# Linformer attention and a hard-swish feed-forward layer: key and value projections in two column tiles of the array

**Chip, cores, metric.** One Trainium2 chip (trn2), one core. The metric is the device time of one execution in microseconds, as the median of the executions of a kernel.

## The reference, cut to what matters

```python
# q, k, v: (8 batches, 8 heads, 1024 positions, 64); E, F: (64, 1024); fp32 in and out
k_proj = np.einsum('ks,bhsd->bhkd', E, k)          # 1024 positions -> 64
v_proj = np.einsum('ks,bhsd->bhkd', F, v)
attn = softmax(q @ k_proj.transpose(0, 1, 3, 2) / 8)
x = (attn @ v_proj)                                # -> (8192, 512)
h = x @ w_in                                       # 512 -> 2048
out = (h * np.clip(h + 3, 0, 6) / 6) @ w_out       # 2048 -> 512
```

## The kernel before

It computes in bf16. The attention of batch b+1 is a generator. The feed-forward layer of batch b calls it for one step after every group of four first-layer matmuls (called F below; not the matrix F) and after every group of sixteen second-layer matmuls (called S). The order of the steps is thereby the order of TensorE's instructions.

```python
ef_t = consts.tile([P, 2, SO, 2, KP], bf16, name="ef_t")   # E^T, F^T, each twice: 128 columns
...
def attention(b, xT):
    ...
    def project(e, src):
        ps = pat()                                   # one PSUM bank, from a ring of 4
        for so in range(SO):                         # SO = 8, KP = 64
            nc.tensor.matmul(ps, ef_t[:, e, so].rearrange("p a m -> p (a m)"), src[:, :, so, :],
                             start=(so == 0), stop=(so == SO - 1))
            if so == SO // 2 - 1:
                yield
        res[e] = ps
    res = {}
    yield from project(0, kt)
    kp = att.tile([KP, H, 2, D], bf16, tag="kp", name="kp")
    k_ps = res[0].rearrange("p (h d) -> p h d", h=H)
    for a in range(2):
        nc.vector.tensor_copy(kp[:, :, a, :], k_ps[:KP])
    yield
    yield from project(1, vt)
    vp = att.tile([P, H, D], bf16, tag="vp", name="vp")
    nc.vector.tensor_copy(vp.rearrange("p h d -> p (h d)"), res[1])
    yield
    kt_ps = pat().bitcast(bf16)[:, :H * KP]
    ...                                              # 8 transposes of kp, 2 copies into kbd
    yield
    ...                                              # q_transpose(0), scores(0), ..., values, normalise
...
for t in range(NB):                                  # NB = 2, in each batch
    ...
    for fo in range(FO):                             # FO = 16
        first_group(xT, t, g, fo)                    # F: 4 matmuls, a Relu, a VectorE product
        next(steps, None)
        if prev is not None and fo % SB == SB - 1:   # SB = 4
            second_group(*prev, fo // SB)            # S: 16 matmuls, a copy, a store
            next(steps, None)
```

The softmax here doesn't subtract the row's maximum and nothing guards it: scores larger than these inputs give would overflow.

## Time and profile before

| | before |
|---|---|
| median time | 575.63 us (574.79 to 576.09, 3 runs) |
| TensorE busy | 532.7 us of a span of 573.1 us |
| 16 projection matmuls of a steady batch | 3.45 us |
| period of a steady batch | 66.26 us |

The *period* is the time from the first projection matmul of one batch to that of the next. It is 66.26 us five times in a row (from 103.05 to 434.35 us). The profile has no records for some 50 of the feed-forward matmuls, which shows as a count of 3 where the program has 4 and costs no time. The profile's lines are shown in the prediction. Their numbers (in brackets those of the changed kernel, where they differ): L126 the projections, L145 (L142) the transposes of kp, L159 (L156) those of q, L163 (L160) the copy into qT, L169 (L166) the scores, L177 (L174) the denominators and values, L214 (L211) F, L217 and L218 (L214 and L215) its Relu and product, L223 (L220) S. A row of the timeline has start and length in us, engine, line, operation, and the idle time ahead of it with what ended it. PE is TensorE, PEld its weight loads, DVE VectorE, ACT ScalarE and POOL GpSimd; 128*64 are the rows and columns of the array that a matmul uses. A mean duration of a matmul in the groups (381 ns) is not its cost: matmuls overlap, and what counts is the step from one start to the next, 0.216 us at full clock.

### The profile page before, as it was taken

To read this page: it belongs to the slowest core of one execution; us is meant where nothing else is said; L and a number is where in the kernel's file an instruction comes from. 1 tells how busy PE (TensorE), PEld (TensorE's weight loads), DVE (VectorE), ACT (ScalarE), POOL (GpSimd) and SP (SyncE) were. 2 spreads that over 40 slices of the span, in tenths; PEclk is the share of its full clock that TensorE was granted. 3 is DMA by queue.
4 is the path that set the end of the run, shared out by engine and by line. 5 is a ranking of instruction groups with operands and counts; after the bars stand their busy time and mean duration, and the time that the engine had idled before them with its cause. 6 is when DMAs were issued, how large, how long until landed. Compare 5 with 4: busy or idle time off the path is not lost.

```text
span 573.1 us, 7173 instructions
## 1 busy us (share of the span) xinstructions
PE 532.7 (93%) x2770; PEld 240.3 (42%) x2824; DVE 254.4 (44%) x400; ACT 302.9 (53%) x513; POOL 28.9 (5%) x40
## 2 busy tenths in 40 slices
PE   2656999999999999999999999999999999999997
PEld 1212444444444444444444444444444444444443
DVE  1342764354535454535544454345444544444420
ACT  0261876366644665356743576437653666544431
POOL 6221000100001000100001000000000000000000
PEclk9887999999999999999999999999999999999999
DMA  9999992552419150380507333000110000011011
GB/s 137 207 206 207 209 214 70 96 106 51 97 38 157 46 102 28 68 153 19 111 37 119 84 74 75 37 20 37 38 37 19 38 37 20 38 51 40 38 38 74
DMA packets 38595, 46.87 MB, mean 82 GB/s; under 512 B 1568, under 2 KB 30240, under 8 KB 38560
## 3 DMA queue, kind: packets, MB, share of 16 engines
q0 software_dynamic: 29344, 29.62, 32.8%
q1 hardware_dynamic: 9216, 16.78, 7.6%
q8 instruction: 22, 0.36, 0.3%
q14 instruction: 13, 0.11, 0.1%
HBM read 59.24 MB, written 16.78 MB: 133 GB/s over the span
## 4 chain that ended last, share of the span: by engine, by line
PE 86%; DMA 8%; DVE 2%; ACT 1%; issue 1%; POOL 1%; ACTq 0%; POOLq 0%
PE mm L223 38%; PE mm L214 37%; DMA v<-in_v_dram 4%; PE at L126 4%; DMA w_in_sb<-in_moe_w_in_dram 4%; PE at L177 3%; PE at L169 2%; PE at L159 2%; DVE g L218 1%; ACT r L217 1%; DVE qT L163 1%; PE at L145 0%; POOL v L78 0%; POOL q L78 0%; POOL k L78 0%
## 5 line engine op out<-in xcount | busy, mean ns | idle before, releaser
L218 DVE SCALAR_TENSOR_TENSOR g<-r,mm 128x512 bf16<-128x512 f32 x256 | 175.5, 686 | 227.4 <-ACT r L217 226.8
L214 PE MATMUL mm<-xT,w_in_sb 128*128 128x512 bf16 x982 | 241.2, 381 | 3.0 <-DVE xT L193 1.0
L223 PE MATMUL mm<-w_out_sb,g 128*128 128x512 bf16 x1012 | 230.0, 379 | 0.6
L217 ACT ACTIVATE r<-mm,half 128x512 f32<-128x512 f32 x256 | 176.8, 691 | 73.6 <-PE mm L214 72.0
L223 PEld LDWEIGHTS <-g 128*128 128x128 bf16 x1024 | 99.8, 98 | 119.3
L214 PEld LDWEIGHTS <-w_in_sb 128*128 128x128 bf16 x1024 | 96.6, 98 | 120.3 <-issue 13.1
L226 ACT COPY o_sb<-mm 128x512 f32<-128x512 f32 x64 | 37.5, 587 | 164.7 <-PE mm L223 161.9
L193 DVE TENSOR_TENSOR xT<-at,rec 128x512 bf16<-128x512 f32 x64 | 43.5, 685 | 22.1 <-ACT rec L192 22.1
L170 ACT ACTIVATE aT<-at 128x512 bf16<-128x512 f32 x64 | 35.0, 609 | 25.6 <-PE at L169 25.6
L192 ACT ACTIVATE rec<-ln 128x512 f32<-128x512 f32 x64 | 40.6, 641 | 0.0
L187 ACT ACTIVATE ln<-at 128x512 f32<-128x512 f32 x64 | 34.6, 596 | 2.2 <-PE at L177 2.2
L126 PE MATMUL at<-k,ef_t 128*128 128x512 bf16 x64 | 18.8, 426 | 14.4 <-DMA k<-in_k_dram 14.4
L163 DVE COPY qT<-at 128x1024 bf16<-128x1024 bf16 x32 | 22.0, 686 | 16.4 <-PE at L159 16.2
L126 PEld LDWEIGHTS <-ef_t 128*128 128x128 bf16 x128 | 13.2, 104 | 36.1 <-issue 11.5
L169 PE MATMUL at<-qT,kbd 128*128 128x512 bf16 x64 | 19.9, 387 | 6.8 <-DVE qT L163 6.2
L159 PE MATMUL at<-ident,q 128*128 128x128 bf16 x256 | 20.0, 222 | 3.2 <-DVE xT L193 1.7
L159 PEld LDWEIGHTS <-q 128*128 128x128 bf16 x256 | 17.2, 99 | 12.0 <-issue 3.5
L126 PE MATMUL at<-v,ef_t 128*128 128x512 bf16 x64 | 17.7, 407 | 1.7 <-DMA v<-in_v_dram 1.5
L177 PE MATMUL at<-aT,ones 64*64 64x512 bf16 x128 | 14.2, 406 | 1.3 <-ACT aT L170 1.1
L177 PE MATMUL at<-aT,vp 64*64 64x512 bf16 x128 | 14.8, 385 | 0.2
L78 POOL DMA_DIRECT2D k<-in_k_dram x8 | 7.0, 881 | 140.6 <-PE at L126 137.0
L78 POOL DMA_DIRECT2D q<-in_q_dram x8 | 7.0, 880 | 140.1 <-PE at L159 136.0
(27 smaller groups left out, 63.3 us busy)
## 6 DMA issues: line engine op xcount, KB each, us to landing
out_dram<-o_sb SPq DMA_DIRECT2D x64, 256.0 KB, 2.0
k<-in_k_dram POOLq DMA_DIRECT2D x8, 1024.0 KB, 9.7
v<-in_v_dram POOLq DMA_DIRECT2D x8, 1024.0 KB, 12.9
q<-in_q_dram POOLq DMA_DIRECT2D x8, 1024.0 KB, 11.1
w_in_sb<-in_moe_w_in_dram POOLq DMA_DIRECT2D x4, 512.0 KB, 21.9
w_out_sb<-in_moe_w_out_dram POOLq DMA_DIRECT2D x4, 512.0 KB, 24.4
ef_raw<-in_E_dram POOLq DMA_DIRECT2D x1, 128.0 KB, 3.0
ef_raw<-in_F_dram POOLq DMA_DIRECT2D x1, 128.0 KB, 3.0
```

Source lines behind the costliest of these rows:

```text
L126: nc.tensor.matmul(ps, ef_t[:, e, so].rearrange("p a m -> p (a m)"), src[:, :, so, :], start=(so == 0), stop=(so == SO - 1))
L159: nc.tensor.transpose(ps[:, o:o + P], qt[:, 2 * j + a, 2 * m:2 * m + 2, :].rearrange("p s d -> p (s d)"), ident)
L170: nc.scalar.activation(aT[j][:, a, :], ps, AF.Exp, scale=scale)
L177: nc.tensor.matmul(tiles[t][c:c + D], stationary(r, 2 * j + a), aT[j][r:r + KP, a, :], start=True, stop=True)
L187: nc.scalar.activation(lns[t], den[t], AF.Ln)
L192: nc.scalar.activation(rec, ln, AF.Exp, scale=-1.0)
L193: nc.vector.tensor_mul(xT[:, j, t, :], av, rec)
L214: nc.tensor.matmul(h_ps, w_in_sb[:, ko, fo * P:(fo + 1) * P], xT[:, ko, t, :], start=(ko == 0), stop=(ko == KO - 1))
L217: nc.scalar.activation(r, h_ps, AF.Relu, bias=half[:], scale=1.0 / 6.0)
L218: nc.vector.scalar_tensor_tensor(g[:, fo, :], r, 1.0, h_ps, op0=ALU.min, op1=ALU.mult)
L223: nc.tensor.matmul(o_ps, g[:, fo, c * P:(c + 1) * P], w_out_sb[:, fo, :], start=(fo == 0), stop=(fo == FO - 1))
L226: nc.scalar.copy(o_sb, o_ps)
```

## The change

The stationary operand of a projection was E or F twice, 128 columns wide, so that the result lay in both halves of the partitions. Now it is 64 columns wide. k's result goes to partitions 0 to 63 and v's to 64 to 127 of one bank, by two column tiles (columns 0 to 63 and 64 to 127 of the array) that are meant to run at the same time. vp, which must be in both halves, is copied twice. One step falls away.

```diff
-    ef_t = consts.tile([P, 2, SO, 2, KP], bf16, name="ef_t")
+    ef_t = consts.tile([P, 2, SO, KP], bf16, name="ef_t")
 ...
     for e in range(2):
-        for a in range(2):
-            nc.vector.tensor_copy(ef_t[:, e, :, a, :], ef_pv[:, e])
+        nc.vector.tensor_copy(ef_t[:, e], ef_pv[:, e])
 ...
-        (project(e, src), its two calls, k_ps, and vp with its copy, as above)
+        ps = pat()
+        for so in range(SO):
+            for e, src in enumerate((kt, vt)):
+                nc.tensor.matmul(ps[e * KP:(e + 1) * KP], ef_t[:, e, so, :], src[:, :, so, :],
                                  start=(so == 0), stop=(so == SO - 1))
+            if so == SO // 2 - 1:
+                yield
         kp = att.tile([KP, H, 2, D], bf16, tag="kp", name="kp")
+        vp = att.tile([P, H, D], bf16, tag="vp", name="vp")
+        k_ps = ps[:KP].rearrange("p (h d) -> p h d", h=H)
+        v_ps = ps[KP:].rearrange("p (h d) -> p h d", h=H)
         for a in range(2):
-            nc.vector.tensor_copy(kp[:, :, a, :], k_ps[:KP])
+            nc.vector.tensor_copy(kp[:, :, a, :], k_ps)
+        for a in range(2):
+            nc.vector.tensor_copy(vp[a * KP:(a + 1) * KP], v_ps)
+        yield
         yield
```

More of the change, by code (lines that the diff above doesn't have):

```diff
@@ L121, in attention @@
         kb = kbd[b % 2]
-        def project(e, src):
-            ps = pat()
-            for so in range(SO):
-                nc.tensor.matmul(ps, ef_t[:, e, so].rearrange("p a m -> p (a m)"), src[:, :, so, :],
+        ps = pat()
+        for so in range(SO):
+            for e, src in enumerate((kt, vt)):
+                nc.tensor.matmul(ps[e * KP:(e + 1) * KP], ef_t[:, e, so, :], src[:, :, so, :],
                                  start=(so == 0), stop=(so == SO - 1))
-                if so == SO // 2 - 1:
-                    yield
-            res[e] = ps
-        res = {}
-        yield from project(0, kt)
+            if so == SO // 2 - 1:
+                yield
         kp = att.tile([KP, H, 2, D], bf16, tag="kp", name="kp")
-        k_ps = res[0].rearrange("p (h d) -> p h d", h=H)
+        vp = att.tile([P, H, D], bf16, tag="vp", name="vp")
+        k_ps = ps[:KP].rearrange("p (h d) -> p h d", h=H)
+        v_ps = ps[KP:].rearrange("p (h d) -> p h d", h=H)
         for a in range(2):
-            nc.vector.tensor_copy(kp[:, :, a, :], k_ps[:KP])
+            nc.vector.tensor_copy(kp[:, :, a, :], k_ps)
+        for a in range(2):
+            nc.vector.tensor_copy(vp[a * KP:(a + 1) * KP], v_ps)
         yield
-        yield from project(1, vt)
-        vp = att.tile([P, H, D], bf16, tag="vp", name="vp")
-        nc.vector.tensor_copy(vp.rearrange("p h d -> p (h d)"), res[1])
         yield
```

## The prediction

> **What bounds the kernel now.** I read the page's busy times first, then the slices, the chain that ended last, the groups, and then the timeline of TensorE in three places: a steady stage, one visit to the array's small tiles, and the start.
>
> ```profile
> PE 532.7 (93%) x2770; PEld 240.3 (42%) x2824; DVE 254.4 (44%) x400; ACT 302.9 (53%) x513; POOL 28.9 (5%) x40
> ...
> PE   2656999999999999999999999999999999999997
> ...
> PEclk9887999999999999999999999999999999999999
> ...
> PE 86%; DMA 8%; DVE 2%; ACT 1%; issue 1%; POOL 1%; ACTq 0%; POOLq 0%
> ```
>
> TensorE is busy from the fifth slice to the end; the chain is 86% TensorE and 8% DMA, the latter all at the start. So from about 53 us on, a microsecond taken from TensorE is one taken from the end, unless a wait takes its place; before that, transfers rule.
>
> ```profile
> L126 PE MATMUL at<-k,ef_t 128*128 128x512 bf16 x64 | 18.8, 426 | 14.4 <-DMA k<-in_k_dram 14.4
> L126 PE MATMUL at<-v,ef_t 128*128 128x512 bf16 x64 | 17.7, 407 | 1.7 <-DMA v<-in_v_dram 1.5
> ```
>
> These are the projections: 16 matmuls for each of 8 batches. The mean durations overlap, so I take the step between starts instead. A steady batch, in the timeline:
>
> ```profile
> 231.25 3.62 PE L223 MATMUL mm<-w_out_sb,g 128*128 128x512 bf16 x16
> 234.70 1.03 PE L214 MATMUL mm<-xT,w_in_sb 128*128 128x512 bf16 x4
> 235.57 1.03 PE L126 MATMUL at<-k,ef_t 128*128 128x512 bf16 x4
> 236.43 1.03 PE L214 MATMUL mm<-xT,w_in_sb 128*128 128x512 bf16 x4
> ...
> 246.82 1.03 PE L214 MATMUL mm<-xT,w_in_sb 128*128 128x512 bf16 x4
> 248.63 0.59 PE L169 MATMUL at<-qT,kbd 128*128 128x512 bf16 x2 [0.79 <-DVE qT L163]
> ```
>
> Sixteen L223 take 3.45 us to the next row: 0.216 us a matmul. Four L126 take 0.86, the same. A batch's 16 projections are 3.45 us. The last row is the only steady wait of size: four L214 should take 0.86 but the scores come 1.81 us later, so 0.95 us per batch is lost waiting for VectorE's copy of qT.
>
> The small tiles are already used by the denominators and values (L177), 64 rows by 64 columns:
>
> ```profile
> 188.00 0.59 PE L223 MATMUL mm<-w_out_sb,g 128*128 128x512 bf16 x2
> 188.52 0.41 PE L177 MATMUL at<-aT,ones 64*64 64x512 bf16 x4
> 188.76 0.39 PE L177 MATMUL at<-aT,vp 64*64 64x512 bf16 x4
> 189.08 0.60 PE L214 MATMUL mm<-xT,w_in_sb 128*128 128x512 bf16 x2
> ```
>
> Four matmuls cost one wave of 0.24 us. The L223 pair should end its turn at 188.00 + 2 x 0.216 = 188.43; the small tiles start at 188.52, so entering costs 0.09 us. The second wave needs 0.32 instead of 0.216, so leaving costs 0.10. In each wave, two of the four matmuls share rows of the array and a PSUM bank, and differ in column tile and moving data: just what the change does.
>
> **What the Trainium skill says.** "TensorEngine Tiling (Array Packing)", Key Properties: tiles work independently, and changing the tiling mode drains TensorE. The rows above agree: 4 in one wave, 0.09 and 0.10 us for the changes. "TensorE: Matmul & The Clock Gate", Part 3, The mechanism: weight loads overlap running matmuls only where the row group differs. The trace disagrees:
>
> ```profile
> 188.52 0.11 PEld L177 LDWEIGHTS <-ones 64*64 64x64 bf16 x4 [0.42 <-issue]
> 188.55 0.12 PEld L177 LDWEIGHTS <-vp 64*64 64x64 bf16 x4
> ```
>
> The second wave's weights load at 188.55, under the first wave's matmuls on the same tiles, 0.21 us ahead of use. So I expect the loads of the pairs hidden too. "PSUM — Partial Sum Buffer", The four PSUM rules: accumulation groups in different quadrants of one bank are independent, so two open groups in halves of one bank are sound; L177 has no accumulation, so no row of this trace shows it. The clock page's Part 1 says that the array runs at half clock after idling and recovers after about 3.4 us of activity. The trace agrees: granted clock 0.58 between 37 and 53.3 us, and L126 stepping 0.43 us at 48.2.
>
> **The change part by part.** The order of instructions of both kernels shows how the steps fall between the first layer's groups of four matmuls (F, 0.86 us) and the second layer's groups of sixteen (S, 3.45 us).
>
> 1. Steady projection. Each half is now four pairs: 0.09 to enter, 0.24 for the first wave, two of 0.216, 0.32 for the last with leaving: 1.08 us, against 1.73 for eight matmuls. Two halves: 1.29 us saved per batch.
>
> 2. Shifted steps. An attention now takes 29 steps instead of 30, so all behind the projection comes one step earlier. The qT0 transposes move behind an S, which leaves VectorE 3.45 us to clear its queue. Scores then wait for one 0.69 us copy behind a 0.86 us F: I leave 0.1 of the 0.95 us.
>
> 3. New waits. The kp copies (2 x 0.67 us) follow the second half, and their transposes come after two F (1.73 us). VectorE first finishes an L218 about 0.55 us after the half, so kp is ready at 0.55 + 1.35 + 0.05 = 1.95: 0.2 us lost. The first value quads lose the S that stood ahead of them: the copy of qT1 comes behind two exponentials and an L218, and frees a PSUM tile of the quads about 0.35 us late. Together 0.55.
>
> 4. vp becomes two half copies: one more of 0.67 us per batch on VectorE (44% busy), off the path but for the kp queue counted.
>
> Net for a steady batch: 1.29 + 0.85 - 0.55 = 1.6 us. Attentions 2 to 7 are steady: 6 x 1.6 = 9.5 us.
>
> 5. The start takes some back. Batch 0's attention is done at about 39 us and TensorE then waits for transfers, so its projection saves nothing; it now starts with v at 17.3 us, ends perhaps 1.4 us later, and that is hidden. Batch 1 is not hidden:
>
> ```profile
> 27.62 25.67 DMA v<-in_v_dram
> ...
> 53.33 1.04 PE at L126 x4
> ```
>
> v lands at 53.3, k at 48.2. Before, TensorE used the 5 us between for all of k's projection and two F, which also woke the clock. Now the second matmul of the first pair waits for v with everything behind it. From 53.3 on the old order has 1.73 us of v left; the new one has 2.16 of pairs and two more F (1.73): 2.2 us more. The clock is still low, and until it recovers (3.4 to 5 us) half the time is lost: some 2 us. Together about 4 us later, where the early VectorE queue may add or hide one.
>
> Sum: 575.6 - 9.5 + 4 = about 570.
>
> **Rivals.** A: the start costs little (the clock recovers at once, or VectorE and ScalarE set the pace in batch 0's first layer anyway, where each F needs 0.69 us of both): the net is 566 to 567. For it: the page gives L218 and L217 on the early chain. Against: TensorE is above 95% busy from 53.3 to 110 us. B: the pairs do not overlap, because each uses all 128 rows or because both accumulate into one bank: 16 x 0.216 plus four mode changes, 0.4 us more than before per batch. With step 2 and 3 about even and the start 5 us worse: about 580. Against: the L177 rows, where two streams on the same rows and bank run together. C: weight loads without the 128-column form are exposed, some 0.03 us per matmul or 0.24 per half: this eats 0.5 us per batch, giving 573. Against: the loads at 188.55. D: new waits are larger than my 0.55, because VectorE holds vp's copies ahead of L218 at a crowded moment: each 0.3 us costs 2 us in all, 572. E: they vanish: 567.
>
> **Range and chances.** The steady gain may be 1.1 to 2.0 us per batch (7 to 12 in all), the start's cost 2 to 6, and runs differ by about 0.6. I take 570 with 566 to 574.5. Faster by 2% means under 564.1, which needs the whole steady gain and no cost at the start: 4%. Slower by 2% means over 587, more than B: 2%.
>
> **What would show it.** Pairs start within 0.01 us of each other and waves step 0.216 us; a half takes 1.08. From one batch's projection to the next takes 64.7 us where it took 66.26. The wait of L169 for qT falls from 6.2 us in all to under 2. TensorE stands idle from 40 to 53 us, but for one matmul at 48, and the first second-layer group comes at about 80 us instead of 76.4. I am wrong if pairs step 0.43 us, if kp's transposes wait over 0.5 us, or if the first second-layer group is not late.

## The result

The changed kernel takes 566.87 us (566.23 to 568.04, 4 runs) against 575.84 us (574.79 to 576.09, 4 runs). The ratio is 0.985, with an interval of 0.983 to 0.987. The 9 us are well clear of noise.

From the page after: the busy times, TensorE's slices, the chain by engine, and the two groups of the projections.

```profile
PE 523.7 (93%) x2824; PEld 234.5 (42%) x2824; DVE 257.5 (46%) x406; ACT 301.2 (53%) x513; POOL 28.9 (5%) x40
...
PE   1552899999999999999999999999999999999997
...
PE 89%; DMA 8%; POOL 1%; DVE 1%; ACT 0%; issue 0%; ACTq 0%; POOLq 0%
...
L126 PE MATMUL at<-k,ef_t 128*64 128x512 bf16 x64 | 19.6, 431 | 13.5 <-DMA k<-in_k_dram 13.5
L126 PE MATMUL at<-v,ef_t 128*64 128x512 bf16 x64 | 19.1, 430 | 9.0 <-DMA v<-in_v_dram 9.0
```

TensorE is busy for 9 us less, and its idle share is what it was; with 54 matmul records missing before and none after, this is no exact count. But the k and v groups look as busy as before (19.6 and 19.1 us against 18.8 and 17.7): each is busy while the other is, so a group's busy time hides the overlap. VectorE's 6 more instructions are 8 more vp copies less 2 of ef_t. The projections now wait 9.0 us for v, at the start.

**Steady state.** The timeline of TensorE in a batch after:

```profile
236.21 0.40 PE L126 MATMUL at<-k,ef_t 128*64 128x512 bf16 x1
236.22 0.40 PE L126 MATMUL at<-v,ef_t 128*64 128x512 bf16 x1
236.45 0.38 PE L126 MATMUL at<-k,ef_t 128*64 128x512 bf16 x1
236.46 0.38 PE L126 MATMUL at<-v,ef_t 128*64 128x512 bf16 x1
...
240.99 0.41 PE L142 MATMUL at<-ident,kp 64*128 64x64 bf16 x8
241.32 3.63 PE L220 MATMUL mm<-w_out_sb,g 128*128 128x512 bf16 x16
244.79 0.61 PE L156 MATMUL at<-ident,q 128*128 128x128 bf16 x8
245.23 1.03 PE L211 MATMUL mm<-xT,w_in_sb 128*128 128x512 bf16 x4
246.18 0.59 PE L166 MATMUL at<-qT,kbd 128*128 128x512 bf16 x2
```

k and v start 0.01 us apart, and the pairs step by 0.24 us once and 0.216 then. The qT transposes (L156) now come after an S, and the scores (L166) follow their F after 0.95 us instead of 1.81, with no wait shown. The view by stretches shows one period before and one after:

```profile
103.05:169.31 66.26, 65.10 (x347) 29.62 (x353) 31.39 (x49) 37.52 (x64) 2.63 (x3) 1.00 0.40 80
```

```profile
107.98:172.10 64.12, 64.12 (x354) 28.77 (x354) 31.81 (x50) 37.29 (x64) 2.62 (x3) 1.00 0.42 83
```

The second number is the length, the third TensorE's busy time. Before, 1.16 us were idle, 0.79 of it the wait of the scores and the rest next to records that are missing; now nothing is idle. The period fell by 2.14 us. Six attentions (2 to 7) gain it: 12.8 us.

**Start.** Yet the second batch's projection begins at 107.98 instead of 103.05 us: 4.9 us are given back. The timeline after, around v's landing (not all pairs shown):

```profile
48.51 0.64 PE L126 MATMUL at<-k,ef_t 128*64 128x512 bf16 x1 [7.16 <-DMA k<-in_k_dram]
53.63 0.58 PE L126 MATMUL at<-v,ef_t 128*64 128x512 bf16 x1 [4.49 <-DMA v<-in_v_dram]
...
55.43 1.57 PE L211 MATMUL mm<-xT,w_in_sb 128*128 128x512 bf16 x4
56.93 0.40 PE L126 MATMUL at<-k,ef_t 128*64 128x512 bf16 x1
...
64.53 0.59 PE L166 MATMUL at<-qT,kbd 128*128 128x512 bf16 x2 [2.09 <-DVE qT L160]
```

The first scores before:

```profile
60.55 0.59 PE L169 MATMUL at<-qT,kbd 128*128 128x512 bf16 x2 [0.69 <-DVE qT L163]
```

One k matmul runs at 48.5 us and TensorE stands until v lands at 53.6 us; the kernel before did eight k matmuls and eight of F in that time. From v's landing to batch 2 it is 54.35 us, against 49.72 before (103.05 - 53.33). I account for these 4.63 us as follows. Two F and the slower projection (2.16 us of pairs where 1.73 us of v was left) are 2.16. The first half of the pairs takes 1.80 instead of 1.08 us and its F 1.50 instead of 0.86, at half clock: 1.36. By the steps the first scores come 2.25 us later than their F alone would have them, instead of 0.86 us (the rows show 2.09 and 0.69 of idle), and 0.27 us of a wait for q is gone: 1.1. VectorE works with no pause of note from 58.36 to 64.47 us, and the copy of qT ends last: ahead of it stand both copies of kp (1.27 us) and of vp (1.40, where one took 0.68), three products and the two copies into kbd. The sum is 4.6.

The two traces differ by luck too: the one before got its full clock back at 51.0 us, 2.8 us after k's landing. The shift alone (below), which projects batch 1 at full width too, got it back at 54.4 us, 5.9 us after k's landing. By the medians the start costs 12.8 - 9.0 = about 4 us.

### The profile page after: what moved, and what is told of

It reads as the page before. It is cut to its first block, busy times and chain, and to the rows that moved or that the text cites. A ratio compares the mean times of both kernels' runs of the same rounds, so it can differ in the third digit from the quotient of the medians.

```text
span 565.1 us, 7227 instructions
## 1 busy us (share of the span) xinstructions
PE 523.7 (93%) x2824; PEld 234.5 (42%) x2824; DVE 257.5 (46%) x406; ACT 301.2 (53%) x513; POOL 28.9 (5%) x40
## 4 chain that ended last, share of the span: by engine, by line
PE 89%; DMA 8%; POOL 1%; DVE 1%; ACT 0%; issue 0%; ACTq 0%; POOLq 0%
PE mm L220 39%; PE mm L211 39%; DMA v<-in_v_dram 5%; DMA w_in_sb<-in_moe_w_in_dram 4%; PE at L174 3%; PE at L126 3%; PE at L166 2%; PE at L156 2%; PE at L142 0%; DVE g L215 0%; DVE qT L160 0%; ACT r L214 0%; POOL v L78 0%; POOL q L78 0%; POOL k L78 0%
## 5 line engine op out<-in xcount | busy, mean ns | idle before, releaser
L126 PE MATMUL at<-k,ef_t 128*64 128x512 bf16 x64 | 19.6, 431 | 13.5 <-DMA k<-in_k_dram 13.5
L126 PE MATMUL at<-v,ef_t 128*64 128x512 bf16 x64 | 19.1, 430 | 9.0 <-DMA v<-in_v_dram 9.0
L166 PE MATMUL at<-qT,kbd 128*128 128x512 bf16 x64 | 20.0, 390 | 3.8 <-DVE qT L160 3.5
L126 PEld LDWEIGHTS <-ef_t 128*64 128x64 bf16 x128 | 7.2, 118 | 35.6 <-issue 22.9
L156 PE MATMUL at<-ident,q 128*128 128x128 bf16 x256 | 20.4, 225 | 1.7 <-DVE xT L190 1.7
L156 PEld LDWEIGHTS <-q 128*128 128x128 bf16 x256 | 17.7, 101 | 10.2 <-issue 3.5
L135 DVE CAST kp<-at 64x512 bf16<-64x512 f32 x16 | 10.2, 675 | 14.3 <-PE at L126 14.3
```

What stands on the lines that cost most here:

```text
L126: nc.tensor.matmul(ps[e * KP:(e + 1) * KP], ef_t[:, e, so, :], src[:, :, so, :], start=(so == 0), stop=(so == SO - 1))
L156: nc.tensor.transpose(ps[:, o:o + P], qt[:, 2 * j + a, 2 * m:2 * m + 2, :].rearrange("p s d -> p (s d)"), ident)
```

## The experiments

My theory after the result: (1) pairs overlap, for 1.27 us a batch; (2) the shift by one step takes away the scores' wait of 0.87 us; (3) the start loses 4 to 5 us as k waits for v. Rivals: all of the gain is (1) or all (2); the narrow weights or the bank matter; the start's loss has another cause. Four, four and three kernels shared runs of the kernel before, with medians of 575.84, 576.27 and 575.71 us. All results were correct. The three ran on three chips, and the changed kernel was not run again in them, so a difference to its 566.87 us is uncertain by about the 0.56 us between those three medians.

| kernel | median us | ratio to before | period us |
|---|---|---|---|
| before | 575.84 | 1 | 66.26 |
| changed | 566.87 | 0.985 | 64.12 |
| one more empty step | 571.97 | 0.9926 | 64.99 |
| shift alone, full width | 570.59 | 0.9904 | 65.39 |
| batch 1 k first, column tiles | 564.73 | 0.980 | 64.12 |
| not alternating | 567.11 | 0.9849 | 64.14 |
| two banks | 567.57 | 0.9851 | 64.12 |
| vp copied first | 576.23 | 1.0005 | 65.59 |
| surplus matmuls ahead of v | 566.32 | 0.9833 | 64.12 |
| one column tile for both | 578.36 | 1.0043 | 65.83 |
| eight pairs in one step | 564.72 | 0.9815 | 63.89 |
| batch 1 at full width | 562.67 | 0.9779 | 64.12 |
| the last two together | 561.22 | 0.9752 | 63.89 |

### One more empty step

```diff
         yield
         yield
+        yield
         kt_ps = pat().bitcast(bf16)[:, :H * KP]
```

> The changed kernel with one more empty step ahead of the transposes of kp, so that everything behind the projection lies where it lay before. Theory (overlap of pairs 1.27 us per batch, and 0.87 us from the scores' wait that the shift removed): the batch period goes from 64.12 to about 65.0 us, the wait of the scores for qT comes back, and the time rises by 6 x 0.87 = 5 us to about 572. Rival (the wait went because the vp copies or the single PSUM bank changed VectorE's queue, not because of the step): the period stays at 64.1 and the time at 567.

The timeline has the wait back, 0.79 us of idle as in the kernel before:

```profile
249.71 0.59 PE L167 MATMUL at<-qT,kbd 128*128 128x512 bf16 x2 [0.79 <-DVE qT L161]
```

Period and time came as the theory said: 64.99 us, and 5.1 us slower than the changed kernel. VectorE's queue behind the pairs is the same, so it is the place of the step that made and removed the wait.

### The shift alone

```diff
         nc.vector.tensor_copy(vp.rearrange("p h d -> p (h d)"), res[1])
-        yield
         kt_ps = pat().bitcast(bf16)[:, :H * KP]
```

(The kernel before, with nothing else changed.)

> The kernel before, full-width projections, with only the kp transposes moved one step earlier, so that 29 steps remain. Theory: the wait of the scores goes without any column tile: period 66.26 to about 65.4, time 575.8 - 5 = about 570.6. Rival (all of the gain is the pairs' overlap): no change, 575.8.

```profile
246.42 0.59 PE L168 MATMUL at<-qT,kbd 128*128 128x512 bf16 x2
```

No wait is shown any more, the period is 65.39 (0.87 less), the time 5.25 us less. So 0.87 of the 2.14 us a batch has nothing to do with column tiles: 5 us could be had by taking out one line. The rest, 65.39 - 64.12 = 1.27, is the pairs; six times that, less the start's 4 us, leaves them some 3.6 of the net 9 us.

### Both projections in one column tile

```diff
-        ps = pat()
+        pse = [pat(), pat()]
 ...
-                nc.tensor.matmul(ps[e * KP:(e + 1) * KP], ef_t[:, e, so, :], src[:, :, so, :],
+                nc.tensor.matmul(pse[e][:KP], ef_t[:, e, so, :], src[:, :, so, :],
 ...                                                  # k_ps = pse[0][:KP], v_ps = pse[1][:KP]
```

> The changed kernel with both projections in the first column tile (partitions 0 to 63) of two banks, so the same narrow weights, order and steps, but one tile. Theory (the gain of the pairs is the overlap of two column tiles): 16 matmuls follow each other every 0.216 us, 0.86 us more per half, period 64.12 + 1.73 = about 65.9, time about 577 less what the start hides: 576 to 578. Rival (narrow weights or the alternation of k and v are what is faster): under 570. If narrow weight loads are exposed in one tile, the step shows it as over 0.216.

```profile
240.23 0.40 PE L126 MATMUL at<-k,ef_t 128*64 128x512 bf16 x1
240.47 0.38 PE L126 MATMUL at<-v,ef_t 128*64 128x512 bf16 x1
240.69 0.38 PE L126 MATMUL at<-k,ef_t 128*64 128x512 bf16 x1
```

In one tile each matmul waits its turn, at the same 0.216 us as full-width ones. The period of 65.83 is that of the shift alone plus 0.44 for the changes of mode, and with the start's loss on top the kernel is slower than before (578.36 us, 0.4 over the range I gave). So the two column tiles are the gain; narrow weights neither help nor hurt.

### Not alternating

```diff
-        for so in range(SO):
+        for part in range(2):
             for e, src in enumerate((kt, vt)):
+                for so in range(part * SO // 2, (part + 1) * SO // 2):
```

> The changed kernel with each half issued as four k matmuls and then four v matmuls, in the same two column tiles and bank. Theory (matmuls of one tile follow each other every 0.216 us, only neighbours in the queue overlap, and start in order of issue): a half takes 7 waves instead of 4, so 0.65 us more per half, period 65.4, time about 566.9 + 6 x 1.3 - up to 1 (four k matmuls run before v lands) = 573 to 575. Rival (TensorE runs the two tiles independently, each with its own queue, whatever the order): no change, 567.

My theory was wrong here, and the rival right. In a half of a steady batch, with four k matmuls issued ahead of four v matmuls, the timeline is

```profile
237.66 0.40 PE L127 MATMUL at<-k,ef_t 128*64 128x512 bf16 x1
237.67 0.40 PE L127 MATMUL at<-v,ef_t 128*64 128x512 bf16 x1
237.90 0.38 PE L127 MATMUL at<-k,ef_t 128*64 128x512 bf16 x1
```

The first v starts 0.01 us after the first k, though three k matmuls stand ahead of it. That the k matmuls do stand ahead is seen in batch 1 of the same trace, where four run at 49.07 us and the four v at 54.19, when v has landed. So a column tile takes its next matmul past at least three that wait for the other tile. A matmul that waits for a transfer is not passed: in the changed kernel the second k matmul stood behind the first v until 53.64 us. The alternate issue of the change is not needed for its gain.

### Two banks

```diff
-        ps = pat()
+        pse = [pat(), pat()]
 ...
-                nc.tensor.matmul(ps[e * KP:(e + 1) * KP], ef_t[:, e, so, :], src[:, :, so, :],
+                nc.tensor.matmul(pse[e][e * KP:(e + 1) * KP], ef_t[:, e, so, :], src[:, :, so, :],
 ...                                                  # k_ps = pse[0][:KP], v_ps = pse[1][KP:]
```

> The changed kernel with k's and v's projections accumulating in two PSUM banks, still in the two column tiles. Theory (one bank for both tiles costs nothing): pairs start within 0.01 us, waves step 0.216 us, period 64.12, time within 0.5 us of the changed kernel's 566.9. Rival (writes of two accumulations to one bank hinder each other a little): waves shorter than now and a faster kernel; the opposite is also possible if one more tile of the ring of four brings a new wait, and would show as an idle ahead of a row of the timeline.

The period is the same 64.12 and the ratio 0.9851 against 0.985. The median is 0.7 us above the changed kernel's, just outside what I had written, but the kernel before was 0.4 us slower in those rounds too. The single bank costs nothing and saves a tile of the ring.

### vp copied first

```diff
-        for a in range(2):
-            nc.vector.tensor_copy(kp[:, :, a, :], k_ps)
         for a in range(2):
             nc.vector.tensor_copy(vp[a * KP:(a + 1) * KP], v_ps)
+        for a in range(2):
+            nc.vector.tensor_copy(kp[:, :, a, :], k_ps)
```

> The changed kernel with the two copies of vp ahead of the two of kp on VectorE. In the changed kernel the copies of kp end 0.1 us ahead of the transposes that need them. Theory (that slack is some 0.1 us and no more): kp is ready 1.2 to 1.3 us later, TensorE waits 1.1 to 1.3 us ahead of the transposes in each batch, period about 65.3, time 566.9 + 6 x 1.2 = about 574. Rival (the slack is of the size of a whole VectorE instruction or more, which is why the 0.2 us that I predicted did not show): under 0.7 us per batch, 571 or less.

```profile
246.19 0.40 PE L142 MATMUL at<-ident,kp 64*128 64x64 bf16 x8 [1.41 <-DVE kp L137]
```

The kp copies end 4.24 us after the half's first pair instead of 2.70, so 1.54 us later, and 1.47 us a batch becomes a wait. That is more than the 1.1 to 1.3 expected, and with the start's loss it undoes the whole gain in time (576.23 us). So the slack of the changed kernel here is 0.1 us or less. That the new wait of my prediction did not appear was a near thing.

### Batch 1 alone, k ahead of v in column tiles

```diff
+        pv = pat() if b == 1 else ps
 ...
+        if b == 1:                    # k in two steps, copies of kp, v in two steps, copies of vp
+            ...
+        else:                         # pairs, as in the change
+            ...
```

> The changed kernel, but batch 1 alone projects k in two steps and then v in two steps, not in pairs, each in its own column tile and bank. Theory (batch 1's pairs wait for v and leave TensorE idle from 41 to 53.6 us, which costs some 4.8 us against the kernel before): the second attention's successor starts its projection at about 103 to 104 us instead of 108, the period stays 64.12, and the time is about 562.3. Rival (the late start is made by VectorE's longer queue or by a later v transfer, whatever the order): at most 1.5 us faster, 565.5 or more.

It gained 2.1 us (2.9 by the ratios), half of what I expected; in its trace batch 2 starts at 106.28 us. The order of k and v was not all of it, or something new came with it: single matmuls in column tiles still pay for the changes of mode, and vp is still copied twice at a crowded moment. In its trace the clock also came back only at about 54.9 us, 5.9 us after k's landing.

### Surplus matmuls ahead of v

```diff
         ps = pat()
+        if b == 1:
+            for _ in range(11):
+                nc.tensor.matmul(ps[:KP], ef_t[:, 0, 0, :], kt[:, :, 0, :], start=True, stop=True)
```

> The changed kernel with eleven surplus matmuls of k's first slice ahead of batch 1's pairs, in the time that TensorE waits for v (48.5 to 53.6 us), so that the clock has had 3 to 5 us of work when v lands. Results are the same, for the first real matmul restarts the accumulation. Theory (of the start's cost about 1.3 us is half clock after v's landing): the first half of pairs and the first four matmuls after v step at 0.216 instead of 0.43 us, and the time falls by 0.7 to 1.4 us, to about 565.8. Rival (the pace after v is set by ScalarE and VectorE, which the clock does not slow): no change, 566.9.

```profile
53.75 0.38 PE L129 MATMUL at<-v,ef_t 128*64 128x512 bf16 x1 [0.58 <-DMA v<-in_v_dram]
53.76 0.40 PE L129 MATMUL at<-k,ef_t 128*64 128x512 bf16 x1
53.97 0.38 PE L129 MATMUL at<-v,ef_t 128*64 128x512 bf16 x1
...
63.27 0.59 PE L169 MATMUL at<-qT,kbd 128*128 128x512 bf16 x2 [2.09 <-DVE qT L163]
```

In the profiled execution the pairs step 0.21 us right from v's landing, and batch 2 comes 52.97 us after it instead of 54.35: 1.38 us less, the 1.36 of the account above. The scores' wait of 2.09 us is the same at full clock, so it is a term of its own. By the medians only 0.55 us is gained (by the ratios, 0.0017 of 576 = 1.0), within my bounds of 0.7 to 1.4 by one measure and not by the other. The size of the clock's part in the typical execution stays open to half a microsecond or so, as its time of recovery varies.

### Eight pairs in one step

```diff
-            if so == SO // 2 - 1:
-                yield
 ...
         yield
         yield
+        yield
         kt_ps = pat().bitcast(bf16)[:, :H * KP]
```

> The changed kernel with all eight pairs in one step and one more empty step behind, so that everything from the kp transposes on lies where it does now. Theory (each entry into and exit from the column tiles costs 0.09 + 0.10 us and the first wave 0.02 more): one entry and exit fewer per batch, period 64.12 - 0.21 = about 63.9, time 6 x 0.21 = 1.3 us less, about 565.6. The kp copies have one more group of four matmuls to hide behind. Rival (the changes of mode are an artefact of how ends are modelled, or 2.0 us of pairs in one block delay ScalarE's and VectorE's feed): period 64.1 or more, 566.9 or more.

The period is 63.89, so 0.23 us less for one entry and one exit of the tiles fewer, as 0.09 + 0.02 + 0.10 had it. The time is 2.1 us less; 1.4 of it is the six periods. The rest is at the start: in the traces batch 2 begins 58.71 us after k's landing instead of 59.47.

### Batch 1 at full width, and both together

```diff
+            if b == 1:
+                nc.tensor.matmul((ps, pv)[e], ef_t[:, e, so].rearrange("p a m -> p (a m)"), src[:, :, so, :],
+                                 start=(so == 0), stop=(so == SO - 1))
+            else:                                     # column tiles; ef_t holds E and F twice again
+                ...
```

> The changed kernel, but batch 1 alone projects as the kernel before does: full width, k in two steps, then v in two steps, vp by one copy. The run with batch 1 in separate column tiles gained 2.1 us of the some 4 us that the start costs. Theory (what was left there is four changes of tiling mode, 0.8 us, and VectorE's longer queue ahead of the first scores, about 1 us): the rest of the start's cost goes too, 566.9 - 4 = about 563.0. Rival (what was left is the time at which the clock recovers, which varies from execution to execution): no better than 564.7.

```profile
53.44 1.03 PE L133 MATMUL at<-v,ef_t 128*128 128x512 bf16 x4
...
59.83 0.59 PE L195 MATMUL at<-qT,kbd 128*128 128x512 bf16 x2
```

562.67 us: 4.2 us less, where 3.9 was expected. k is done when v lands, the scores come at 59.83 us instead of 64.53 with no wait for qT, and batch 2 starts 49.84 us after v, as in the kernel before (49.72). The time is also what the kernel before would take with six periods of 64.12, 575.8 - 12.8 = 563.0. So the start's cost was the way in which batch 1 projects, all of it. What batch 1 in separate column tiles had left is 2.1 us by the medians (1.2 by the ratios), and its parts are not told apart: the tiles' changes of mode, VectorE's queue, and the clock too, which came back 5.9 us after k's landing in that trace and 3.5 us after it in this one, worth 1.2 us by itself.

> Batch 1 at full width as in the run just above, and all other batches with eight pairs in one step. Theory (the two gains are independent): period 63.9, time about 563.0 - 1.3 = 561.7, faster than both kernels, 2.4% under the kernel before. Rival: one of the two gains is absent, 563 to 565.5.

Together they take 561.22 us, a ratio of 0.9752 (0.9738 to 0.9765) to the kernel before. Period 63.89 and start (batch 2 at 103.91 us) both stand. It is the fastest kernel of this study.

## Why the prediction was right

The time, 566.87 us, lies in the range of 566 to 574.5, near its lower end, 3.1 us under the 570 said. The steady gain of 2.14 us a batch lies outside the 1.1 to 2.0 that I gave, and the period is 64.12 us where I said 64.7.

1. *Steady projection, 1.29 us a batch.* Right: 1.27 by the shift alone against the changed kernel. The costs of 0.09, 0.24 and 0.10 us, read from the value matmuls of the kernel before, carried over unchanged to another shape.
2. *Shifted steps, 0.85.* Right: 0.87, and shown alone in both directions.
3. *New waits, 0.55.* This is the term that was mis-sized: it measured 0, and 6 x 0.55 = 3.3 us is the whole difference from 570. For kp I set VectorE's end (1.95 us after the half) against two F of 1.73 us, but left out the 0.10 us of leaving the tiles and the 0.09 of entering the transposes' own tiling, which I had just measured and which delay TensorE too; and I added two copies of 0.67 us where two back to back take 1.27 together. The copies end at 240.87 us and the transposes could start at 240.97. For the value quads, likewise: I added two exponentials of 0.61 where two take 1.08, and the copy of qT1 ended at 249.86, ahead of the quads that need its tile (249.98). Both waits were absent by some 0.1 us or less, as the run with vp first shows for kp.
4. *vp's second copy off the path.* Right in steady state: VectorE rose from 44 to 46%. Not so at the start.
5. *The start, about 4 us.* Right in size: about 4 by the medians, 4.6 in the trace. The order was as told: 2.2 us (2.16). The clock cost less than the some 2 us (1.36), and a third term was missing and only hinted at: a longer wait for qT, 1.1 us. That these two errors nearly cancel is luck. I had written that the wait of L169 would fall under 2 us in all; it is 0 in steady batches but 3.5 us at the start, in two places. The first second-layer group came at 81.1 us, where I said about 80 (before, the timeline has it at 76.25 us; my 76.4 was read from the chain).

Of the rivals, A (the start costs little) named 566 to 567, so the right time for a wrong reason: leaving batch 1 at full width gained 4.2 us. B (no overlap) fell to the timeline and the run in one tile. C (exposed weight loads) fell to the step of 0.216 us. D (larger new waits) fell to steady batches without any. E (the new waits vanish) is what happened, with the 567 I gave it.

## What to carry to other kernels

Before putting two operands into one instruction stream, look at when each arrives: pairing makes the first wait for the last, and here it took back a third of the steady gain, all of it recovered by leaving out the one batch that still waits for its transfers. When a change also moves a step, run the shift alone: here one deleted line was worth 5 of the 9 us. In estimates of a queue use the step between back-to-back instructions, not their durations, and charge a change of tiling mode to everything behind it.

## What the Trainium skill lacked or had wrong

- "TensorE: Matmul & The Clock Gate", Part 3, The mechanism, says that matmuls start and end in strict order, and that weight loads overlap running matmuls only where the row group differs, though the same section also lets loads for a background weight buffer go ahead. Here, with four k matmuls issued ahead of four v matmuls in another column tile, the first v started 0.01 us after the first k and 0.23 us ahead of the second k, which is not strict order; and weights for tiles in use were loading 0.21 us ahead of their turn, which fits the looser of the two statements on loads.
- "TensorEngine Tiling (Array Packing)", Key Properties, has no figure for the drain at a change of mode. Here it is 0.09 us in, 0.10 out and 0.02 in the first wave; saving one visit saved 0.23 us.
- "PSUM — Partial Sum Buffer" says in The four PSUM rules that groups in different quadrants of a bank are independent, and in its section on bank collisions that different column tiles can use one bank at the same time, but gives no time for either. One bank and two gave the same period here, 64.12 us.
